# Gate and value projections of a gated FFN written as Strassen block products over pairs of token chunks

## The chip, the core and the metric

The kernel runs on one core of a Trainium2 chip: one TensorE (PE, with its weight loads PEld), one VectorE (DVE), one ScalarE (ACT), one GpSimd (POOL), and DMA queues fed from SyncE (SP). The metric is the device time of one execution in microseconds. Three executions of the kernel before took 867.61, 870.18 and 871.58 us; the median, 870.18 us, is the time to beat. Faster and slower are meant against a bound of 0.5% (4.35 us).

## What is computed

A hash attention over 2 x 8 heads of 768 tokens, then a softplus FFN, then a gated FFN on 1536 tokens of width 512 with 1536 hidden columns. Only the last is changed:

```python
def _moe2_ref(x, w_gate, w_val, w_out):
    g = x @ w_gate                         # 1536x512 @ 512x1536
    silu = g * (1.0 / (1.0 + np.exp(-g)))
    val = x @ w_val
    return (silu * val @ w_out)            # 1536x1536 @ 1536x512
```

## The kernel before

**Chunks.** The tokens are handled in four chunks c = 0 to 3 of 384 tokens, two for each of the two batches b. Attention gives `xy[c]`, the first FFN (`ffn1`) turns it into the next `xy[c]`, and the gated FFN (`ffn2`) makes the output of that chunk. The hidden width of a chunk lies on partitions (512 = KD x 128, KD = 4), its 384 tokens (CN) on the free axis.

**High and low halves.** Inputs of float32 precision are held as two halves, a rounded one and a remainder. Each 128 x 128 block of a weight meets each 128 x 384 block of data three times (`three`, L1133 to L1136): high by high, high by low, low by high. In gate and value the halves are float16 (L1134, L1135, L1136); in the out-projection they are float32r (L1300, L1301, L1302; 512 columns each). So a chunk takes 12 x 2 x 4 x 3 = 288 matmuls of 384 columns for gate and value and 3 x 12 x 3 = 108 matmuls of 512 columns for the out-projection; the four chunks take 1152 and 432.

**`ffn2`, one chunk.** For each of the 12 blocks m of hidden columns, gate goes into one bank of a PSUM tile z, value into the other. ACT takes the sigmoid (L1262), DVE multiplies by gate and by value (L1268, twice), ACT makes the high half sT (L1274), POOL the low half (L1277). After 12 blocks, three token tiles f are accumulated over all 12 blocks in PSUM, copied (ACT, L1307) and stored. The PSUM rings that matter are z (2 tiles of two banks), y and pv (1 bank each), f (2 banks).

**Weights.** `piece` (L388) loads a float64 array of 128 x 1024 values and turns it into float32 with three DVE instructions (L408, L413, L419, tile w32b); `split16` measures its size (ACT, L446, a square with an accumulated sum), and makes its two halves (L452 or L458, L462); `split32` does the same for the out-projection without a scale (L486, L490). The 12 pieces of gate and value are all made before `ffn2` starts, the 6 pieces of the out-projection in its first 40 us.

**`ffn1`'s end.** Four tiles y of 128 x 384 leave PSUM for `xy[c]` in two steps, the high half by ACT (`hi`, L1228), the low half by DVE from the same bank (`lo`, L1233).

**The order.** Every piece of work is a `step` with an engine or several (`ways`), a cost, an urgency, the steps it follows, and ring slots it takes and uses. `Order.run` (L128) walks through time by these costs, places the step that can start first (the lowest urgency among those within 0.1067 us), and so fixes each engine's queue, which the chip then runs strictly in that order. A change of steps in one place can move rows elsewhere on every engine.

## Time and profile before

| | |
|---|---|
| median of three executions | 870.18 us (867.61 to 871.58) |
| the profiled execution, first to last instruction | 868.9 us |
| PE busy | 818.3 us, 94% of the span |
| DVE, ACT, POOL busy | 546.1, 441.7, 356.9 us |
| start of gate and value | 577.24 us |
| last matmul starts | 864.71 us |

The profiled execution's time outside its span is not listed; its span lies 1.3 us below the median and inside the range of the three. A PE row's duration holds the whole passage of a matmul through the array, and the next one starts long before it ends; so what a matmul costs in a stream is read from the distance between two starts, not from its duration. Idle time of the other engines costs nothing unless PE waits for them.

### The profile page before, as it was taken

What the parts mean: (1) busy time and instruction counts of PE and PEld (TensorE: products, weight loads), DVE (VectorE), ACT (ScalarE), POOL (GpSimd) and SP (SyncE); (2) the same over time, 40 slices, a digit from 0 to 9 for tenths busy, and PEclk for the clock granted to TensorE, in tenths of its full rate; (3) what the DMA queues carried; (4) which work ended last, traced back from release to release, by engine and by line L of the source; (5) the groups of instructions that cost most, each with busy time, mean ns of one, the idle gap of its engine ahead of it and who ended that gap; (6) DMA issues with size and microseconds to landing.
All of it is one profiled execution on the core that took longest, in us unless ns stands there. A gap on an engine that the chain in (4) does not pass through costs nothing. (4 is left out here: it accounts for less than half of the span.)

```text
span 868.9 us, 14539 instructions
## 1 busy us (share of the span) xinstructions
PE 818.3 (94%) x5576; PEld 530.4 (61%) x5576; DVE 546.1 (63%) x1018; ACT 441.7 (51%) x845; POOL 356.9 (41%) x361
## 2 busy tenths in 40 slices
PE   7999898889989899788999999999999999999998
PEld 3667666545555555455666666555686686677666
DVE  4778896879998678888558789889602301311220
ACT  3445465568788578885778458534302211211220
POOL 0001201669787769986778317413301201210220
PEclk9979999999999999999999999999999999999999
DMA  6224433776859896566683650445000000001001
GB/s 205 71 86 150 149 98 103 170 139 127 199 108 171 160 174 127 113 123 113 126 151 58 206 191 5 143 160 183 1 24 13 2 24 13 1 1 37 1 1 37
DMA packets 179269, 86.10 MB, mean 99 GB/s; under 512 B 141120, under 2 KB 165888, under 8 KB 179200
## 3 DMA queue, kind: packets, MB, share of 16 engines
q1 hardware_dynamic: 179200, 85.17, 41.5%
q8 instruction: 44, 0.72, 0.4%
q14 instruction: 25, 0.20, 0.1%
HBM read 47.35 MB, written 3.15 MB: 58 GB/s over the span
## 5 line engine op out<-in xcount | busy, mean ns | idle before, releaser
L1268 DVE SCALAR_TENSOR_TENSOR sg<-z,smalls,sg 128x384 f32<-128x384 f32 x96 | 59.2, 616 | 176.2 <-ACT sg L1262 174.7
L1277 POOL TENSOR_TENSOR sT<-sg,sT 128x384 fp32r<-128x384 f32 x48 | 51.3, 1069 | 213.5 <-ACT sT L1274 202.1
L929 POOL TENSOR_TENSOR P<-E,P 128x768 f16<-128x768 f32 x72 | 124.5, 1730 | 23.3 <-ACT P L916 19.8
L869 PE MATMUL z<-k,q 128*128 128x384 f32 x192 | 79.5, 543 | 3.3 <-DVE E L888 3.3
L1194 POOL TENSOR_TENSOR g<-fr,g 128x384 f16<-128x384 f32 x64 | 71.3, 1116 | 14.9 <-ACT g L1185 11.3
L1134 PE MATMUL f<-xy,w1h 128*128 128x384 f16 x192 | 62.6, 326 | 4.0 <-DVE fr L1163 1.5
L1134 PE MATMUL z<-xy,wgh 128*128 128x384 f16 x192 | 62.6, 326 | 2.1 <-DVE sg L1268 2.1
L909 ACT ACTIVATE E<-E,st 128x768 f32<-128x768 f32 x48 | 44.7, 931 | 37.3 <-DVE E L888 35.3
L1134 PE MATMUL z<-xy,wvh 128*128 128x384 f16 x192 | 62.6, 326 | 0.0
L1135 PE MATMUL z<-xy,wvh 128*128 128x384 f16 x192 | 62.6, 326 | 0.0
L1136 PE MATMUL z<-xy,wvl 128*128 128x384 f16 x192 | 62.6, 326 | 0.0
L1136 PE MATMUL z<-xy,wgl 128*128 128x384 f16 x192 | 62.6, 326 | 0.0
L1135 PE MATMUL z<-xy,wgh 128*128 128x384 f16 x192 | 62.6, 326 | 0.0
L1136 PE MATMUL f<-xy,w1l 128*128 128x384 f16 x192 | 62.6, 326 | 0.0
L1135 PE MATMUL f<-xy,w1h 128*128 128x384 f16 x192 | 62.6, 326 | 0.0
L1262 ACT ACTIVATE sg<-z,smalls 128x384 f32<-128x384 f32 x48 | 27.8, 580 | 64.2 <-PE z L1136 62.8
L966 PEld LDWEIGHTS <-PT 128*128 128x128 f16 x1296 | 46.5, 99 | 22.0 <-DMA PT<-P 12.2
L1180 DVE SCALAR_TENSOR_TENSOR fr<-fa,smalls,fr 128x384 f32<-128x384 f32 x64 | 54.4, 852 | 5.2 <-ACT fa L1177 2.3
L966 PE MATMUL pv<-v,PT 128*128 128x64 f16 x1296 | 50.2, 194 | 7.8 <-DMA PT<-P 4.9
L1300 PE MATMUL f<-woh,sT 128*128 128x512 f32 x144 | 56.6, 393 | 0.0
L1274 ACT ACTIVATE sT<-sg 128x384 fp32r<-128x384 f32 x48 | 25.0, 522 | 61.0 <-DVE sg L1268 61.0
L1301 PE MATMUL f<-wol,sT 128*128 128x512 f32 x144 | 56.1, 389 | 0.0
(207 smaller groups left out, 2036.6 us busy)
## 6 DMA issues: line engine op xcount, KB each, us to landing
raw64a<-in_moe_w_in_dram SPq DMA_DIRECT2D x16, 512.0 KB, 4.6
raw64a<-in_moe_w_out_dram SPq DMA_DIRECT2D x16, 512.0 KB, 5.0
raw64b<-in_moe_w_gate_dram SPq DMA_DIRECT2D x12, 512.0 KB, 4.4
raw64b<-in_moe_w_val_dram SPq DMA_DIRECT2D x12, 512.0 KB, 4.9
raw64b<-in_moe_w_out_dram SPq DMA_DIRECT2D x12, 512.0 KB, 4.0
rawk<-in_k_dram SPq DMA_DIRECT2D x19, 192.0 KB, 2.9
rawv<-in_v_dram SPq DMA_DIRECT2D x19, 192.0 KB, 3.0
rawq<-in_q_dram SPq DMA_DIRECT2D x16, 192.0 KB, 3.1
```

The lines of the kernel that those rows point to most:

```text
L869: nc.tensor.matmul(a[:, x, 0:HS], lhsT=plain(qd["q"])[:, ts], rhs=plain(kd["k"])[:, x * HS:(x + 1) * HS], start=True, stop=True,)
L929: return lambda: eng.tensor_tensor(P.t[:, 1, :], E.t.rearrange("p a b -> p (a b)"), P.t[:, 0, :], op=ALU.subtract)
L966: nc.tensor.matmul(pv.t[:, t, :], lhsT=PT.t[:, w, kk, :], rhs=values.t[:, kk, c0:c0 + D], start=(kk == 0 and w == 0 and c0 == 0), stop=(kk ...
L1134: nc.tensor.matmul(ps, lhsT=wh, rhs=xh, start=first, stop=False)
L1135: nc.tensor.matmul(ps, lhsT=wh, rhs=xl, start=False, stop=False)
L1136: nc.tensor.matmul(ps, lhsT=wl, rhs=xh, start=False, stop=last)
L1180: nc.vector.scalar_tensor_tensor(out=fr.t, in0=fa.t, scalar=sc[b]["sg"], in1=fr.t, op0=ALU.mult, op1=ALU.add)
L1194: return lambda: eng.tensor_tensor(g.t[:, 1], fr.t, g.t[:, 0], op=ALU.subtract)
L1268: return lambda: nc.vector.scalar_tensor_tensor(out=sg.t, in0=z.t[:, j, 0:CN], scalar=gvs[b, "gv"[j]][:, gi:gi + 1], in1=sg.t, op0=ALU.mul ...
L1277: return lambda: eng.tensor_tensor(sT.t[:, 1, :], sg.t, sT.t[:, 0, :].bitcast(F32), op=ALU.subtract)
L1300: nc.tensor.matmul(ps, lhsT=s[:, 0, cs], rhs=wh, start=(kk == 0), stop=False)
L1301: nc.tensor.matmul(ps, lhsT=s[:, 0, cs], rhs=wl, start=False, stop=False)
```

## The change

`ffn2` is replaced by `pair_of`, which handles the two chunks of a batch (p = 0, 1) and two blocks of hidden columns (mp = 0 to 5) at once: a 2 x 2 block product for gate and one for value. Each is made from 7 products (p1 to p7 in the code) instead of 8. A product is 6 matmuls of 384 columns (2 blocks of depth x `three`). The sums that go with it are made in four places.

- **Of the data, once for each batch** (`parts7`): `ffn1`'s y is kept as float32 in one step (`keep_a` or `keep_v`). Then 8 squares with sums on ACT, a total, 4 scalings, 4 subtractions and 7 splits into halves, all on arrays of 128 x 768.
- **Of the weights, for each of 12 pieces** (`split7`): 4 sums of 128 x 256 on POOL (tile sw), and the halves of 2048 instead of 1024 values. The pieces live in a ring of 4 (w7), those of the out-projection in a ring of 2 (wo); so from mp = 2 on they are made while `pair_of` runs.
- **Of the products.** Each of gate and value has a PSUM tile A of ring z (two banks, a and c) and one bank more, y or pv. In bank a, p1, p6, p7 and p4 are added one upon the other, and after each of the first three ACT copies the running sum out to SBUF (`keep`, tile cc). Bank c takes p5 and later p3, the third bank p2. DVE adds a bank to a copy (`plus`: c11, c22, c12). So p6 waits for the first copy, p7 for the second, p4 for the third, p3 for c22.
- **Of the output.** A pair's out-projection covers two hidden blocks only (6 matmuls for each of 6 token tiles), and is added to an array acc in SBUF (DVE; 12 first copies by ACT and DVE, 60 adds). It is issued behind the products of a later pair. The stores come with mp = 5.

A pair is thus 14 products and 6 out-products of 6 matmuls each. There are 12 pairs, in the order (0,0), (0,1), (1,0), (1,1), (0,2), (1,2) and so on; all of it counts 1008 matmuls of 384 columns and 432 of 512.

```diff
+        "raw64a": 1, "w32a": 2, "raw64b": 2, "w32b": 2, "sw": 1, "w7": 4, "wo": 2,
+        "fa": 2, "fr": 2, "g": K1, "cc": 10, "sg": 4, "sT": 8,
     }
     order = Order(RINGS)
...
+    def yf(c):
+        return xy[c].rearrange("p a k n -> p (a k n)").bitcast(F32).rearrange("p (k n) -> p k n", k=KD)
...
-            def hi(mt=mt, y=y):
+            def keep_a(mt=mt, y=y):
...
-            def lo(mt=mt, y=y):
...
-            a = step(U["f1"], "A", act(CN), hi, [s, y_ready], uses=[y])
-            done.append(step(U["f1"], "V", stt(CN), lo, [a], uses=[y]))
-        return done
...
+            last.append(s)
+            done.append(ways(U["f1"], [("A", act(CN), keep_a), ("V", dve(CN) + 0.13, keep_v)], [s, y_ready], uses=[y]))
+        return done, last
...
+    def parts7(p, opened, y_ready):
...
+        def sub(o, x, y, after):
+            def go(eng):
+                return lambda: eng.tensor_tensor(f[o](), f[x](), f[y](), op=ALU.subtract)
+            return ways(u, [("W", dve(n) + 0.05, go(nc.vector)), ("G", gps(n) + 0.15, go(nc.gpsimd), BV["lo"])], after)
...
+            s = ways(u, [("A", act(n), hi_a), ("G", gts(n) + 0.08, hi_g), ("W", dve(n, 2), hi_v)], after)
+            s = ways(u, [("G", gps(n) + 0.05, lo(nc.gpsimd)), ("W", dve(n) + 0.07, lo(nc.vector))], [s])
...
+        u = -1.0 if p else 200.0
...
+        s11, s21, s12, s22 = (scaled(j) for j in ("11", "21", "12", "22"))
+        b11, b21, b22 = halves("11", [s11] + after), halves("21", [s21] + after), halves("22", [s22] + after)
+        t1 = sub("t1", "12", "11", [s11, s12] + after)
+        h1 = halves("t1", [t1])
+        t3 = sub("t3", "22", "12", [t1, s22])
+        halves("t3", [t3])
+        t2 = sub("t2", "22", "t1", [h1, s22])
+        h2 = halves("t2", [t2])
+        t4 = sub("t4", "21", "t2", [t2, b21])
+        h4 = halves("t4", [t4])
+        return out, ready, [b11, b22, h2, h4, ready["t3"]], known
...
+            def sums(eng):
...
+                    eng.tensor_tensor(o[:, 0], a21, a22, op=ALU.add)
+                    eng.tensor_tensor(o[:, 1], o[:, 0], a11, op=ALU.subtract)
+                    eng.tensor_tensor(o[:, 2], a11, a21, op=ALU.subtract)
+                    eng.tensor_tensor(o[:, 3], a12, o[:, 1], op=ALU.subtract)
...
+            raw = s
...
+            g = step(due, "-", 0.0, make, [raw], takes=[slot], line="w7")
+            s = step(due, "A", act(n) + 0.24, measure, [g], uses=[w32, slot])
+            s, bank_ = total(due, m, 1, [s])
+            sc_ = step(due, "V", 0.6, scale(bank_), [s], uses=[bank_])
+            sm = ways(due, [("G", 4 * gps(CB) + 0.2, sums(nc.gpsimd)), ("W", 4 * dve(CB) + 0.1, sums(nc.vector), BV["lo"])], [raw],
+                      takes=[sw], uses=[w32])
+            done = []
...
+    def pair_of(p, mp, gw, wo, f2_open, y7, y7_ready):
...
+            def prod(k, wj, name, bank, first, after, takes=(), uses=(), line=None):
+                return step(due + k + 0.5 * i, "E", cost, mult(wj, 0, name, bank, first),
+                            [w_done[wj // 4], y7_ready[name], w_scale[b]] + after, takes=takes, uses=[w7] + list(uses), line=line)
...
+            def keep(slot, after, A=A, sc_=sc_):
+                def go():
+                    nc.scalar.activation(new(late["f2"], [128, CN], F32, slot), A.t[:, 0, 0:CN], AF.Copy, scale=sc_[:, mp:mp + 1])
+                return step(0, "A", act(CN), go, after + [f2_open], takes=[slot], uses=[A], line="cc")
...
+            def plus(slot, bank, after, uses, sc_=sc_):
+                def go():
+                    nc.vector.scalar_tensor_tensor(
+                        out=slot.t, in0=bank(), scalar=sc_[:, mp:mp + 1], in1=slot.t, op0=ALU.mult, op1=ALU.add
+                    )
+                return step(0, "V", stt(CN) + 0.08, go, after, uses=[slot] + uses)
+            s1, u2, u3 = Slot("cc"), Slot("cc"), Slot("cc")
+            p1 = prod(0, 0, "11", bank_a, True, [f2_open], takes=[A], line="u1")
+            p5 = prod(1, 4, "t1", bank_c, True, [p1], uses=[A])
+            k1 = keep(s1, [p1])
+            p6 = prod(2, 5, "t2", bank_a, False, [k1], uses=[A])
+            p2 = prod(3, 2, "21", bank_b, True, [p1], takes=[Bk], line="u2")
+            k2 = keep(u2, [p6])
+            p7 = prod(4, 6, "t3", bank_a, False, [k2], uses=[A])
+            k3 = keep(u3, [p7])
+            c11 = plus(s1, bank_b, [p2, k1], [Bk])
+            c22 = plus(u3, bank_c, [p5, k3], [A])
+            p4 = prod(5, 3, "t4", bank_a, False, [k3], uses=[A])
+            p3 = prod(6, 7, "22", bank_c, False, [c22], uses=[A])
+            c12 = plus(u2, bank_c, [p3, k2], [A])
+            ends[i] = [c11, c12, p4, c22]
+            tiles[i] = [s1, u2, A, u3]
...
+            def mul(eng, t, sg=sg):
+                return lambda: eng.tensor_tensor(sg.t, t.t, sg.t, op=ALU.mult)
+
+            def mul_raw(n, t, sg=sg):
+                return lambda: nc.vector.scalar_tensor_tensor(
+                    out=sg.t, in0=t.t[:, 0, 0:CN], scalar=gvs[b, n][:, mp:mp + 1], in1=sg.t, op0=ALU.mult, op1=ALU.mult
                 )
...
+            for n, t, e in (("g", tg, None), ("v", tv, ends[1][j])):
+                if raw:
+                    s = step(0, "V", stt(CN) + 0.08, mul_raw(n, t), [s, e], uses=[t, sg])
+                else:
+                    s = ways(0, [("W", dve(CN), mul(nc.vector, t), 0.3), ("G", gps(CN) + 0.1, mul(nc.gpsimd, t))], [s, e], uses=[t, sg])
...
+                s = step(due + 105, "E", pe(6 * DM), mm, [pairs[0][1], pairs[1][1], wo_done], takes=[f],
+                         uses=[pairs[0][0], pairs[1][0], wo_slot])
...
+                if mp == 0:
+                    s = ways(0, [("V", dve(DM), first_v), ("A", act(DM) - 0.08, first_a)], [s], uses=[f])
+                else:
+                    s = step(0, "V", dve(DM) + 0.1, add, [s, sums_of[c, i]], uses=[f])
+                sums_of[c, i] = s
+                if mp == NG2 - 1:
+                    step(0, "D", (0.7, 0.73), store, [s])
...
+    f2_open = step(0, "-", 0.0, open_f2, [s for c in range(NCH) for s in y_last[c]])
...
+    turns_of = [(0, 0), (0, 1), (1, 0), (1, 1)]
+    turns_of += [(p, mp) for mp in range(2, NG2) for p in range(B)]
+    for p, mp in turns_of:
+        pair_of(p, mp, gws[mp], wos[mp], f2_open, y7[p], y7_ready[p])
```

What the queues become is shown at two places. The first is DVE's queue as gate and value start. Before, it holds the rest of the last weight piece (w32b, wvl), four scale steps, two pieces of the out-projection, and the multiplications of the first blocks (sg):

```order
L462 SCALAR_TENSOR_TENSOR wvl_5924<-w32b_1185_6826,smalls_87,wvh_5923 128x4x256
L1420 TENSOR_SCALAR smalls_87<-smalls_87 128x6 x4
L408 TENSOR_SCALAR w32b_1191_6928<-raw64b_1189_6922 128x1024
L413 SCALAR_TENSOR_TENSOR w32b_1191_6928<-raw64b_1189_6922,w32b_1191_6928 128x1024
L419 SCALAR_TENSOR_TENSOR w32b_1191_6928<-raw64b_1189_6922,w32b_1191_6928 128x1024
L408 TENSOR_SCALAR w32b_1194_6959<-raw64b_1190_6925 128x1024
L1268 SCALAR_TENSOR_TENSOR sg_1193_6957<-z_1188_6897,smalls_87,sg_1193_6957 128x384
L413 SCALAR_TENSOR_TENSOR w32b_1194_6959<-raw64b_1190_6925,w32b_1194_6959 128x1024
L1268 SCALAR_TENSOR_TENSOR sg_1193_6957<-z_1188_6897,smalls_87,sg_1193_6957 128x384
```

Now the same place holds the second batch's data sums (xy2 and xy3 are its two chunks, ty a scratch array), whose first instruction is the reduction L1309 eight rows ahead of these. The first `plus` of a product bank (cc) comes behind them:

```order
L1274 TENSOR_TENSOR ty_5907<-xy3_2434,xy2_2433 128x768
L1290 TENSOR_TENSOR xy0_131<-xy2_2433,xy0_131 128x768 x2
L1274 TENSOR_TENSOR xy3_2434<-xy3_2434 128x768
L1675 TENSOR_SCALAR smalls_87<-smalls_87 128x1
L1676 TENSOR_TENSOR smalls_87<-smalls_87 128x1
L1675 TENSOR_SCALAR smalls_87<-smalls_87 128x1
L1676 TENSOR_TENSOR smalls_87<-smalls_87 128x1
L1675 TENSOR_SCALAR smalls_87<-smalls_87 128x1
L1676 TENSOR_TENSOR smalls_87<-smalls_87 128x1
L1468 SCALAR_TENSOR_TENSOR cc_1174_6843<-y_1177_6867,smalls_87,cc_1174_6843 128x384
L1290 TENSOR_TENSOR xy1_132<-ty_5907,xy1_132 128x768
L1290 TENSOR_TENSOR y3_6816<-xy3_2434,y3_6816 128x768
L1468 SCALAR_TENSOR_TENSOR cc_1180_6898<-z_1171_6818,smalls_87,cc_1180_6898 128x384
```

Counted from L1309, 17 rows now stand ahead of the first cc row: four small ones for the scales, one conversion of a weight piece (L408), two scalings, two casts, and then those shown. Two more rows of 768 values stand between the first cc row and the second.

The second place is PE's queue where one hidden block or pair gives way to the next. Before, value's last matmul of a block is followed by gate's first of the next, which goes to the other slot of ring z:

```order
L1135 MATMUL z_1188_6897<-xy0_131,wvh_5923 128x384
L1136 LDWEIGHTS wvl_5924
L1136 MATMUL z_1188_6897<-xy0_131,wvl_5924 128x384
L1134 LDWEIGHTS wgh_5921
L1134 MATMUL z_1192_6932<-xy0_131,wgh_5921 128x384
L1135 LDWEIGHTS wgh_5921
L1135 MATMUL z_1192_6932<-xy0_131,wgh_5921 128x384
```

Now at the change from pair (0,1) to pair (1,0), the last product of value (z_1206) is followed at once by the first of the next pair, which takes the PSUM tile of gate (z_1189 before it, z_1225 now):

```order
L1135 MATMUL z_1206_7087<-y7_5906,w7_1194_7015 128x384
L1136 LDWEIGHTS w7_1194_7015
L1136 MATMUL z_1206_7087<-y7_5906,w7_1194_7015 128x384
L1134 LDWEIGHTS w7_1085_5995
L1134 MATMUL z_1225_7217<-xy0_131,w7_1085_5995 128x384
L1135 LDWEIGHTS w7_1085_5995
L1135 MATMUL z_1225_7217<-xy0_131,w7_1085_5995 128x384
```

At the change from pair (1,4) to pair (0,5), two out-products (f) stand between, of which the second is shown:

```order
L1537 MATMUL f_1457_8862<-wo_1395_8404,sT_1426_8627 128x512
L1538 MATMUL f_1457_8862<-wo_1395_8404,sT_1426_8627 128x512
L1539 MATMUL f_1457_8862<-wo_1395_8404,sT_1426_8627 128x512
L1537 MATMUL f_1457_8862<-wo_1395_8404,sT_1437_8715 128x512
L1538 MATMUL f_1457_8862<-wo_1395_8404,sT_1437_8715 128x512
L1539 MATMUL f_1457_8862<-wo_1395_8404,sT_1437_8715 128x512
L1134 LDWEIGHTS w7_1398_8437
L1134 MATMUL z_1459_8875<-y7_5906,w7_1398_8437 128x384
```

Ring z has 2 slots and a pair takes both, so the first product of a pair now always waits for the tile of the pair just finished. From pair (0,2) on two or three out-products stand in that place (one ahead of pair (1,2)); none stands ahead of pairs (0,1), (1,0) and (1,1).

## Rows read from the trace of the kernel before

**Rows 1.** The page's first part: busy time, share and instructions by engine.

```profile
PE 818.3 (94%) x5576; PEld 530.4 (61%) x5576; DVE 546.1 (63%) x1018; ACT 441.7 (51%) x845; POOL 356.9 (41%) x361
```

**Rows 2.** Busy time by stretch, from the start of gate and value.

```profile
core 0: us, PE busy (x) PEld busy (x) DVE busy (x) ACT busy (x) POOL busy (x), PEclk, DMA share, GB/s
577.20:587.40 10.20, 8.08 (x52) 4.81 (x51) 9.26 (x18) 3.60 (x5) 1.12 (x1) 1.00 0.30 108
587.40:626.20 38.80, 38.80 (x239) 23.28 (x239) 32.66 (x39) 15.98 (x26) 14.33 (x11) 1.00 0.26 94
...
651.00:865.10 214.10, 214.10 (x1189) 145.02 (x1188) 44.49 (x72) 45.02 (x81) 35.85 (x36) 1.00 0.03 12
```

**Rows 3.** What PE waited for, 440 to 592 us and 380 to 450 us.

```profile
PE z L1134 <- DVE sg L1268: 2.1, 1, 2.1
PE z L1134 <- DVE fr L1163: 1.1, 1, 1.1
...
PE y L1134 <- DVE xy L1233: 3.7, 1, 3.7
```

**Rows 4.** Timeline: gate's first matmul, two streams of matmuls, the end.

```profile
577.24 0.32 PE L1134 MATMUL z<-xy,wgh 128*128 128x384 f16 x1
...
838.00 0.33 PE L1134 MATMUL z<-xy,wgh 128*128 128x384 f16 x1
...
840.27 0.33 PE L1136 MATMUL z<-xy,wvl 128*128 128x384 f16 x1
...
840.90 0.39 PE L1302 MATMUL f<-woh,sT 128*128 128x512 f32 x1
...
849.53 0.39 PE L1301 MATMUL f<-wol,sT 128*128 128x512 f32 x1
...
864.71 0.39 PE L1302 MATMUL f<-woh,sT 128*128 128x512 f32 x1
865.18 0.59 ACT L1307 COPY ob<-f 128x512 f32<-128x512 f32 x1 [7.61 <-PE f L1302]
```

**Rows 5.** Groups by line and shape: busy us, mean ns, idle before them.

```profile
L1268 DVE SCALAR_TENSOR_TENSOR sg<-z,smalls,sg 128x384 f32<-128x384 f32 x96 | 59.2, 616 | 176.2 <-ACT sg L1262 174.7
L413 DVE SCALAR_TENSOR_TENSOR w32b<-raw64b,w32b 128x1024 int32<-128x1024 int32 x18 | 24.2, 1346 | 0.3
L408 DVE TENSOR_SCALAR w32b<-raw64b 128x1024 int32<-128x1024 int32 x18 | 13.8, 767 | 2.0 <-DMA raw64b<-in_moe_w_gate_dram 2.0
L462 DVE SCALAR_TENSOR_TENSOR wvl<-w32b,smalls,wvh 128x1024 f16<-128x1024 f32 x6 | 7.7, 1278 | 0.8 <-POOL wvh L458 0.8
L490 DVE TENSOR_TENSOR wol<-w32b,woh 128x1024 fp32r<-128x1024 f32 x6 | 7.3, 1218 | 0.6 <-ACT woh L486 0.6
L377 DVE TENSOR_SCALAR smalls<-smalls 128x1 int32<-128x1 int32 x12 | 1.8, 153 | 0.4
L1262 ACT ACTIVATE sg<-z,smalls 128x384 f32<-128x384 f32 x48 | 27.8, 580 | 64.2 <-PE z L1136 62.8 <-POOL sT L1277 1.2
L916 ACT CAST P<-E 128x768 f16<-128x768 f32 x44 | 36.3, 826 | 25.4 <-DMA PT<-P 25.1 <-ACT E L909 0.3
L486 ACT ACTIVATE woh<-w32b 128x1024 fp32r<-128x1024 f32 x6 | 6.3, 1055 | 8.8 <-DVE w32b L419 8.8
L446 ACT ACTIVATION_READ_ACCUMULATOR wgh<-w32b 128x1 f32 x6 | 1.1, 187 | 0.0
L1262 ACT ACT_TABLE_LOAD x1 | 1.3, 1283 | 3.5 <-DVE smalls L1420 3.5
L1277 POOL TENSOR_TENSOR sT<-sg,sT 128x384 fp32r<-128x384 f32 x48 | 51.3, 1069 | 213.5 <-ACT sT L1274 202.1 <-issue 11.4
```

**Rows 6.** By tile: shortest, median and longest duration (ns), first and last start.

```profile
L413 DVE SCALAR_TENSOR_TENSOR w32b<-raw64b,w32b x18: 1214/1226/2020, 487.1 to 613.7; 128x1024 int32<-128x1024 int32 x18
L1277 POOL TENSOR_TENSOR sT<-sg,sT x48: 993/994/1625, 588.0 to 843.3; 128x384 fp32r<-128x384 f32 x48
```

**Rows 7.** A stretch in attention with a lower granted clock, columns as in rows 2.

```profile
290.00:300.00 10.00, 7.27 (x51) 4.00 (x50) 5.28 (x14) 5.61 (x13) 6.94 (x8) 0.83 0.87 155
```

346 lines of the change are left out of this document (241 added, 105 removed), and 1 row of the table RINGS.

## Prediction

> **What bounds the kernel now.** I read four views in turn. The page's first part shows PE busy for 94% of the span and no other engine above 63% [rows 1]. An average says little of one stage, so the second view is the busy time by stretch: from 587.4 to 626.2 and again from 651 to the end PE is busy in every microsecond, at the full granted clock (1.00, that is 2.4 GHz), while DVE, ACT and POOL work for only 45, 45 and 36 of the last 214 us [rows 2]. Only the first 10 us of the stage have a gap of 2.1 us: gate's second block waits for a tile that DVE empties [rows 3]. So the stage is a stream of matmuls, and its price is their count by their pitch. The timeline gives the pitch: 14 starts of 384-column matmuls lie 2.27 us apart in all, 0.162 us each, and 38 starts of 512-column ones 8.63 us, 0.227 each [rows 4]. Then 1152 x 0.162 + 432 x 0.227 = 186.9 + 98.1 = 285.0 us, with the gap 287.1; the stage really lasts from 577.24 to the last matmul's end, 864.71 + 0.23 = 864.94, that is 287.7 us [rows 4]. The account closes to 0.6 us. The profiled span is 868.9 us, 1.3 below the median of 870.18; I work out a difference on the span and carry it to the median.
>
> **What is removed.** 144 matmuls of 384 columns of the stage's 1152: 144 x 0.162 = 23.4 us. The out-projection keeps its 432. What is left is 163.5 + 98.1 = 261.6 us. In these units a product is 6 x 0.162 = 0.97 us, an out-product 1.36 us, a pair 14 x 0.97 + 6 x 1.36 = 21.8 us.
>
> **What is mixed.** Out-products now alternate with products, some 72 changes of kind. At one such change the timeline has 0.63 us from the last 384-column start to the third 512-column start, where one step of 0.162 and two of 0.227 make 0.616 [rows 4]; 0.014 us a change gives 1.0 us.
>
> **What is added on the other engines, over some 270 us.** All durations are from the groups [rows 5]; other widths in proportion. DVE: 72 cc sums and 24 multiplications from PSUM at 0.616 (59.2), 27 multiplications of 0.46 (12.3), 60 adds of 512 columns at 0.82 (49.3), 18 low halves at 1.28 (23.0), 14 weight pieces at 0.77 + 2 x 1.35 (48.4; the third instruction is priced as the second), some 63 small ones at 0.153 (9.6), 9 us of the second batch's sums: 211 us. ACT: 168 copies, sigmoids and high halves of 384 columns at 0.58 (97), 30 weight instructions at 1.06 (32), the rest 13: 142 us. POOL: 93 instructions of 384 columns at 1.07 (99.5), 36 weight sums at 0.71 (26), 7 of 1024 columns at 2.85 (20): 145 us. None passes PE's 262, so PE stays the bound on average. What decides is the waits within the chains, which the mean does not show.
>
> **Data sums of the first batch.** Eight squares, a total and some 24 instructions of 768 values, 22 to 27 us of DVE at most. They fall in the time in which PE runs chunk 2's 192 matmuls into y, 31 us, and DVE is relieved there of 8 of the 12 gate and value pieces of 3.46 us. Hidden, 0; without that cover they would cost up to 25 us. ffn1's y now leaves its bank in one step, not two. Before, that bank once waited 3.7 us for the low half behind DVE's queue [rows 3]; I take 1.5 of it back, between 0 and 3.7.
>
> **The entry: the largest stall.** The second batch's sums stand at the head of DVE's queue, and the first cc sums behind them. I count by hand from t = 0, the end of ffn1's last matmul. ACT must still empty the last bank (0.58), split an out-projection piece (1.06) and square (0.77): 2.6 with a hand-off of 0.2 (the end of the old kernel shows 0.24 between PE's last matmul and ACT [rows 4]). PE multiplies three products and the total: 3.1. DVE's four small ones end at 4.0. Then come L408 (0.77), two scalings and two casts (4 x 0.58), four of two inputs (4 x 0.91, from L490's 1.22 for 1024), six small ones (0.93): 11.7. The first cc sum, gate's c11, ends at 12.3. Two low halves follow (14.1), gate's c22 (14.7), value's c11 (15.3), a subtraction (16.2), value's c22 (16.8). Value's last product p3 waits for this one, so pair (0,0) ends at 17.8. Its products are worth 13.6: 4.2 us lost. PE has no other work to put there, since no out-product exists yet.
>
> Pair (0,1) needs the tile of gate, which is free after gate's raw multiplication. DVE still has ahead of that a subtraction and a low half (18.6), gate's c12 (19.2), a low half (20.1), value's c12 (20.7); it ends at 21.4. With the hand-off PE starts at 21.6: 3.8 us more. Within the pair p6 and p7 wait for copies behind sizes and casts on ACT's queue, 0.9 and 1.35. At the turn to (1,0) nothing stands between the last product and the tile's next use: c12 0.62, one piece instruction ahead of it 1.3, raw multiplication 0.62 and the hand-off: 2.7. The turn to (1,1) is spared, since value's p3 stands earlier in its order. (1,2) has one out-product for it: 1.2. Of the eight later turns each has two or three out-products, 2.7 us or more, against a chain of 0.62 + 0.62 + 0.24 and one instruction of DVE that happens to run, 2.1: covered, with 0.6 to spare. A slip of 0.4 each, 3.2. The bounds of these turns: nothing, or 1.3 each (an L413 whole), 10.
>
> **A clock fall.** The stage before never waited. In attention, where PE was busy for 7.27 of 10 us, the granted clock was 0.83 [rows 7], between its two levels (1.2 and 2.4 GHz). The entry has similar gaps. One such stretch costs 0.17 x 10 = 1.7 us; I take one (bounds 0 to 5).
>
> **The end.** The last products' chain is covered by the six out-products of the previous pair, 8.2 us; then an add of 0.82 stands where a copy of 0.59 stood [rows 4], and the stores come in the last 16 us. 0.
>
> **Sum.** Waits: 4.2 + 3.8 + 2.2 + 2.7 + 1.2 + 3.2 + 1.7 = 19.0 (bounds 8 to 30: entry as low as 8 if the casts and pieces run beside each other, as high as 15 with the turns at 10 and the clock at 5). Stage: 261.6 + 1.0 + 19.0 = 281.6 against 287.7, 6.1 less, with y 7.6 less: 870.2 - 7.6 = 863.
>
> **The rivals.**
>
> (A) Slower: DVE and POOL hold each other up. L413 took 1.23 us in the median, 2.02 at the longest; POOL's multiplication 0.99 and 1.63 [rows 6]. POOL goes from 36 us in 214 to 145 in 262, and some 80 DVE instructions have both inputs in SBUF. If that makes the instruction ahead of the release chain 0.8 to 1.5 us longer, each turn loses 1 us or more beyond the 0.6 to spare, and the keeps and cc sums within a pair slip with it. It decides from 7.6 / 12 = 0.6 us a pair; at 1 us a pair the time is 875. Against it: the links themselves (c12, raw multiplication) read one input from PSUM, and such a group, L1268, shows a mean of 616 ns beside a POOL at work [rows 5]. The Trainium skill, "SBUF — State Buffer", section "SBUF: two separate sides", calls the port pair that VectorE (with two SBUF inputs) and GpSimd share an exclusive lock, held for a whole instruction, with the loser blocked. By that rule a DVE instruction could wait a whole 1.07 us; the longest L413 above, 0.8 over its median, agrees with it.
>
> (B) Faster: ACT and DVE run the entry with more overlap than I let them, the turns cost nothing and the clock holds. Waits of 8: 261.6 + 1.0 + 8 = 270.6, 17.1 less, with y 852. For it: the copies and cc sums are short (0.58 and 0.62 us), and DVE and ACT have a third of the stage free; against it: each queue runs strictly in its order, and the entry's order is bad for the cc sums.
>
> (C) No change: the waits eat the gain. Six clock falls of 1.7 in place of one, or turns at 1.3 each, add 8 to 10: 868 to 874. For it: six waits within each pair (copies, cc sums) have a slack of one or two products, 1 to 2 us, less than one weight instruction on ACT (1.06) plus a sigmoid and the table load of 1.28 [rows 5].
>
> **Chances.** The forecast 0.50 with its own range 857 to 869, B 0.20, C 0.17, A 0.13. The bound of 0.5% is 4.35 us, about what a measurement here tells from no change: under 865.8 is faster, over 874.5 slower. Faster: 0.40 of the forecast's half and B, 0.60. Same: 0.10 of the forecast, C and a little of A, 0.29. Slower: the rest of A, 0.11. The range goes from B's 852 to 873; below and above it stay about 2 in 10.
>
> **What would show it.** Right: gate and value start near 577; a pitch of 0.162 and 0.227 unchanged; the first cc sum on DVE some 12 us after the start; PE's waits, some 15 us of them in the first 50 us of the stage, by ACT's and DVE's cc and DVE's sg; later turns with out-products and next to no wait; a clock of 1.00 but for a slice or two. Wrong: waits at every turn, or L413 and POOL's multiplications far longer than here (A); many slices under 1.00 (C); no wait after 590 (B); or a later start of the stage, which would mean that the first batch's sums are not hidden. The likeliest error is in the count of the entry, since each of its steps depends on the one before it.

## The result and the profile after

The changed kernel takes 878.53 us in the median of seven executions (874.79 to 883.32), the kernel before 870.18: the ratio is 1.0100, 95% interval 1.0069 to 1.0131. It is slower by 1%, and lies above the forecast of 863 and above the range's end at 873. The profiled execution took 882.55 us, with a span of 880.6. Ratios and intervals here are made from undisturbed executions alone (one of the run with the first sums late took 1613.9 us and is left out) and can differ by a few thousandths from the ratio of the medians; beside the experiments the kernel before had medians of 868.8 to 870.0.

The first view is the page's first part, against [rows 1]. PE works 6.5 us less, DVE 108 us more.

```profile
PE 811.8 (92%) x5436; PEld 517.1 (59%) x5436; DVE 653.8 (74%) x1188; ACT 501.9 (57%) x966; POOL 473.1 (54%) x453
```

The timeline of PE has the places that answer to [rows 4]: gate's first matmul, the longest wait of the stage with what follows it, and the end.

```profile
586.28 0.33 PE L1134 MATMUL z<-y,w 128*128 128x384 f16 x1
...
605.00 0.33 PE L1136 MATMUL z<-y,w 128*128 128x384 f16 x1
609.45 0.48 PE L1134 MATMUL z<-y,w 128*128 128x384 f16 x1 [4.13 <-DVE sg L1505]
609.73 0.53 PE L1135 MATMUL z<-y,w 128*128 128x384 f16 x1
...
701.82 0.32 PE L1134 MATMUL z<-y,w 128*128 128x384 f16 x1 [1.93 <-DVE cc L1468]
701.98 0.32 PE L1135 MATMUL z<-y,w 128*128 128x384 f16 x1
...
876.44 0.39 PE L1539 MATMUL f<-wo,sT 128*128 128x512 f32 x1
```

Gate and value start 9.0 us later than before (586.28 against 577.24) and last from there to 876.67, 290.4 us against 287.7. So about half of this execution's distance to the forecast lies ahead of the stage. Busy time by stretch (columns as in [rows 2]) shows two stretches ahead of it, then the three that answer to [rows 2], shifted by 9:

```profile
500.00:540.00 40.00, 40.00 (x249) 24.10 (x247) 38.03 (x44) 25.94 (x50) 24.11 (x20) 1.00 0.20 64
560.00:580.00 20.00, 20.00 (x125) 12.05 (x124) 0.16 (x1) 2.39 (x6) 1.43 (x2) 1.00 0.00 1
586.20:596.40 10.20, 9.34 (x60) 5.61 (x59) 6.77 (x14) 7.34 (x12) 5.43 (x2) 1.00 0.01 2
596.40:635.20 38.80, 29.89 (x152) 18.16 (x151) 36.45 (x48) 19.93 (x33) 26.36 (x20) 0.91 0.25 82
660.00:874.10 214.10, 208.01 (x1119) 139.80 (x1118) 159.27 (x242) 91.87 (x163) 117.48 (x106) 1.00 0.15 50
```

DVE is nearly full in 500 to 540 (38.0 of 40 us) and empty in 560 to 580 (0.16 of 20). In the 39 us of the entry PE works only 29.9 us. What PE waited for, first from 451 to 586 us, then in the stage (us in all, times, longest), against [rows 3]:

```profile
PE f L1134 <- DVE smalls L371: 1.4, 1, 1.4
PE f L359 <- DVE fr L1166: 1.3, 1, 1.3
PE f L359 <- ACT w L1354: 1.3, 1, 1.3
PE z L1134 <- DVE fr L1166: 1.0, 2, 0.7
PE pv L966 <- DMA PT<-P: 0.9, 1, 0.9
```

```profile
PE z L1134 <- DVE sg L1505: 6.6, 2, 4.1
PE z L1134 <- DVE cc L1468: 4.2, 5, 1.9
PE z L1134 <- ACT cc L1463: 3.9, 5, 1.2
PE f L1537 <- DVE acc L1553: 2.6, 3, 1.3
PE f L1537 <- DVE acc L1547: 0.7, 1, 0.7
PE f L359 <- ACT w L1354: 0.3, 1, 0.3
```

Counted from start to start, as below, each wait is some 0.17 us longer than its idle time. The stage's 290.4 us are then: matmuls at the pitches of the prediction 262.7 (with ten totals, each two small matmuls that add up the squares of a weight piece), 17 waits 21.3, matmuls at the lower clock 3.2 more than at the full one (12 from 609.45 on and 10 from 637.94 on, each behind a wait of 4.1 and 2.5 us), changes between products and out-products about 1, small rests about 2 (the pitch at 512 columns is 0.230 us here, not 0.227, which makes some 1.2 of them).

### The profile page after: what moved, and what is told of

Read it like the earlier page. It is cut to its first block, busy times and chain, and to the rows that moved or that the text cites. A ratio compares the mean times of both kernels' runs of the same rounds, so it can differ in the third digit from the quotient of the medians.

```text
span 880.6 us, 14652 instructions
## 1 busy us (share of the span) xinstructions
PE 811.8 (92%) x5436; PEld 517.1 (59%) x5436; DVE 653.8 (74%) x1188; ACT 501.9 (57%) x966; POOL 473.1 (54%) x453
## 4 chain that ended last, share of the span: by engine, by line
PE 46%; DVE 27%; DMA 12%; POOL 5%; issue 5%; ACT 3%; SPq 1%; DVEq 0%; POOLq 0%; ACTq 0%
DMA PT<-P 7%; PE z L1134 5%; PE z L1136 5%; PE z L1135 5%; PE z L869 4%; PE f L1537 3%; PE f L1539 3%; PE f L1538 3%; PE f L602 3%; DVE fr L1183 2%; PE pv L966 2%; DMA raw64a<-in_moe_w_in_dram 2%; POOL P L929 2%; DVE E L888 2%; DVE fr L1166 2%
## 5 line engine op out<-in xcount | busy, mean ns | idle before, releaser
L1502 POOL TENSOR_TENSOR sg<-cc,sg 128x384 f32<-128x384 f32 x45 | 51.0, 1144 | 69.8 <-DVE cc L1468 32.9
L1134 PE MATMUL z<-y,w 128*128 128x384 f16 x216 | 71.4, 331 | 12.3 <-DVE cc L1468 4.2
L1197 POOL TENSOR_TENSOR g<-fr,g 128x384 f16<-128x384 f32 x64 | 67.1, 1055 | 17.3 <-ACT g L1188 13.2
L1463 ACT ACTIVATE cc<-z,smalls 128x384 f32<-128x384 f32 x72 | 40.4, 576 | 55.2 <-PE z L1136 54.9
L1513 POOL TENSOR_TENSOR sT<-sg,sT 128x384 fp32r<-128x384 f32 x48 | 59.8, 1263 | 21.4 <-ACT sT L1510 21.4
L1136 PE MATMUL z<-y,w 128*128 128x384 f16 x216 | 71.2, 330 | 0.0
L1135 PE MATMUL z<-y,w 128*128 128x384 f16 x216 | 71.2, 330 | 0.0
L1134 PE MATMUL f<-xy,w1h 128*128 128x384 f16 x192 | 63.9, 333 | 2.5 <-DVE smalls L371 1.4
L1537 PE MATMUL f<-wo,sT 128*128 128x512 f32 x144 | 62.2, 432 | 3.3 <-DVE acc L1553 2.6
L1135 PE MATMUL f<-xy,w1h 128*128 128x384 f16 x192 | 64.0, 333 | 0.0
L966 PEld LDWEIGHTS <-PT 128*128 128x128 f16 x1296 | 47.4, 100 | 25.2 <-DMA PT<-P 15.2
L1539 PE MATMUL f<-wo,sT 128*128 128x512 f32 x144 | 56.4, 392 | 0.0
L1538 PE MATMUL f<-wo,sT 128*128 128x512 f32 x144 | 56.3, 391 | 0.0
L888 DVE TENSOR_SCALAR_CACHE_REDUCE E<-z 128x768 f32<-128x768 f32 x48 | 45.5, 953 | 14.5 <-PE z L869 9.0
L1135 PEld LDWEIGHTS <-w 128*128 128x128 f16 x336 | 33.2, 99 | 36.7 <-issue 18.8
L1553 DVE TENSOR_TENSOR acc<-f,acc 128x512 f32<-128x512 f32 x60 | 41.2, 687 | 16.6 <-PE f L1539 14.9
```

The lines of the kernel that those rows point to most:

```text
L888: nc.vector.tensor_scalar(new(att, [128, 2, HS], F32, E), z.t[:, :, 0:HS], PLAIN_TOP, None, op0=ALU.min, op1=ALU.min, accum_out=a[:, 1:2],)
L966: nc.tensor.matmul(pv.t[:, t, :], lhsT=PT.t[:, w, kk, :], rhs=values.t[:, kk, c0:c0 + D], start=(kk == 0 and w == 0 and c0 == 0), stop=(kk ...
L1134: nc.tensor.matmul(ps, lhsT=wh, rhs=xh, start=first, stop=False, skip_group_check=onto)
L1135: nc.tensor.matmul(ps, lhsT=wh, rhs=xl, start=False, stop=False, skip_group_check=onto)
L1136: nc.tensor.matmul(ps, lhsT=wl, rhs=xh, start=False, stop=last, skip_group_check=onto)
L1197: return lambda: eng.tensor_tensor(g.t[:, 1], fr.t, g.t[:, 0], op=ALU.subtract)
```

## The experiments

All runs are measured by two stretches. The mark between attention and them is the first matmul of the second batch's first FFN into a z tile. Ahead of the mark, five kernels here have the same queues (the changed one, its repetition, the sums later, the filler, no GpSimd products), and yet the mark falls at 451.4, 444.6, 442.9, 452.0 and 446.1 us. That is scatter of attention, and it hides in every total. From the mark on, the changed kernel and its repetition agree within 0.2 us.

| run | mark to gate | stage | both | PE's waits in the stage | median, us | ratio to before (95%) |
|---|---|---|---|---|---|---|
| before | 128.7 | 287.7 | 416.4 | 2.3 | 870.18 | |
| changed | 134.9 | 290.4 | 425.3 | 21.3 | 878.53 | 1.010 (1.007 to 1.013) |
| the same again | 134.9 | 290.6 | 425.5 | 20.9 | 877.29 | 1.009 (1.006 to 1.013) |
| y in two steps | 134.8 | 290.7 | 425.5 | 21.0 | 880.42 | 1.012 (1.004 to 1.019) |
| second sums later | 135.0 | 283.9 | 418.9 | 14.2 | 872.11 | 1.004 (1.000 to 1.008) |
| no sums | 126.0 | 279.2 | 405.2 | 13.4 | 858.66 | 0.983 (0.973 to 0.993) |
| weight sums in four steps | 136.8 | 293.1 | 429.9 | 22.8 | 884.27 | 1.013 (1.004 to 1.022) |
| out-piece later | 145.5 | 287.4 | 432.9 | 19.5 | 884.52 | 1.015 (1.008 to 1.023) |
| three edits | 137.1 | 284.6 | 421.7 | 16.4 | 875.91 | 1.006 (1.001 to 1.010) |
| filler | 135.3 | 288.5 | 423.8 | 14.4 | 877.26 | 1.009 (1.005 to 1.012) |
| first sums late | 131.7 | 286.0 | 417.7 | 18.0 | 870.07 | 1.001 (0.997 to 1.004) |
| both sums late | 129.8 | 285.3 | 415.1 | 15.2 | 870.93 | 1.001 (0.999 to 1.004) |
| pieces late too | 129.2 | 293.6 | 422.8 | 25.3 | 876.69 | 1.011 (1.004 to 1.017) |
| no GpSimd products | 134.7 | 295.4 | 430.1 | 23.2 | 883.32 | 1.016 (1.010 to 1.021) |
| second value piece | 130.6 | 284.3 | 414.9 | 18.3 | 871.83 | 1.005 (1.001 to 1.010) |
| totals later | 129.9 | 288.7 | 418.6 | 22.2 | 872.42 | 1.006 (1.001 to 1.011) |
| both of these | 127.5 | 285.1 | 412.6 | 16.9 | 866.86 | 1.001 (0.997 to 1.005) |
| chain alone | 126.1 | 270.0 | 396.1 | 6.2 | 848.15 | 0.978 (0.973 to 0.984) |

**The same kernel again.**

> The changed kernel once more, unaltered, for a second profile. In the first one gate and value start 9.0 us later than before (586.3 against 577.2) and last 290.4 us against 287.7. If the late start is a property of the order, it comes back within 2 us (584 to 588), and so do the waits of the entry (4.3 us for gate's second tile, 2.7 at the first turn to the second batch). If it was an accident of that execution, the start lies near 578 and the total near 870.

The waits came back one by one, and so did the 134.9 us; the absolute start (579.5) did not, since attention ended 6.8 us earlier. So the first half of the statement holds for the stretch from the mark, and the accident lies ahead of it.

**y in two steps.** Is it the new order of attention's rows?

```diff
-            done.append(ways(U["f1"], [("A", act(CN), keep_a), ("V", dve(CN) + 0.13, keep_v)], [s, y_ready], uses=[y]))
+            def again(mt=mt, y=y):
...
+            a = step(U["f1"], "A", act(CN), keep_a, [s, y_ready], uses=[y])
+            done.append(step(U["f1"], "V", stt(CN), again, [a], uses=[y]))
```

> ffn1's y leaves its bank in two steps again, one of ScalarE and a second of VectorE, whose result goes nowhere. This adds 16 VectorE instructions of about 0.62 us to the changed kernel and gives PE the order of the kernel before up to the first data total at about 492 us. Theory 1, the late start comes from attention's rows being put in another order: the start of the third chunk's first FFN matmuls goes back from 452.6 to about 448.7, and gate and value start 3 to 5 us earlier, at 581 to 583; total 3 to 5 us less than the changed kernel. Theory 2, it comes from the first batch's data sums alone, on VectorE between 490 and 555: 448.7 is not reached again or is given back there, and the total is the same or up to 3 us more.

With PE's old order the stretch takes 134.8 us, as before this edit, so the late start from the mark on is not of that order. The mark lies at 451.2, no earlier, and the median is no lower; given the scatter of the mark, one execution does not exclude a few us ahead of it. The wait for y's bank that the kernel before had ([rows 3], 3.7 us), absent as changed, is back, as the waits from 375 to 450 us show:

```profile
PE y L1134 <- DVE junk L1239: 3.7, 1, 3.7
```

**No sums at all.** The data sums as a whole:

> Left out: all data sums (squares, total, scalings, subtractions, splits of both batches); y leaves as two halves as before, and all seven products take blocks of these halves, so that the output is another one. Everything on the weights, the products and the output stays. It gives the price of the data sums as a whole. If they cause the late start and the slow entry: start at 577 to 580, entry waits under 3 us, total 12 to 18 us under the changed kernel, that is 860 to 866, and what is left of waits belongs to the products' own chain. If the weight pieces and the chain cause the loss: start as late as in the changed kernel, total less than 5 us lower.

Ahead of the stage 8.9 us go, in the stage 11.3, together 20.2, and PE waits for nothing between mark and gate. The total fell by 20, more than expected. With the sums go the 21 one-value multiplications by the data's scale in the stage (L1676), 12.6 us of DVE as changed. The profiled execution is the longest of its four (862.54 us, the median 858.66), but from the mark to the last matmul its clock is 1.00, and the run with the chain alone, below, repeats the 126.0 (126.1). What PE still waited for in the stage:

```profile
PE z L1134 <- ACT cc L1467: 4.1, 4, 1.8
PE f L1541 <- DVE acc L1557: 2.7, 4, 1.0
PE z L1134 <- DVE cc L1472: 2.3, 4, 0.8
PE z L1134 <- DVE sg L1509: 2.1, 2, 1.7
```

**Second batch's sums later.**

```diff
-        u = -1.0 if p else 200.0
+        u = 1.0 if p else 200.0
```

> The second batch's data sums get an urgency below that of the copies and cc sums instead of above. All queues are unchanged up to the end of ffn1. Theory, the entry stands behind these sums on VectorE: the waits inside pair (0,0) (5.1 us) and at the turn to (0,1) (4.3 us) fall to 2 to 4 us together, the stretch at the lower clock behind the second one goes, and the total falls by 5 to 8 us. Rival, the sums are needed anyway and only move: the first pair of the second batch waits for them as long, or the next weight piece comes late, and the total stays within 2 us.

The stage fell by 6.6 us. The 4.3 us at pair (0,1) are gone; a new wait of 3.1 us for value's second weight piece stands 40 us into the stage.

**Weight sums in four steps, and the out-piece later.** Two ways to keep weight work out of the way:

> The four sums of a weight piece become four steps of the planner instead of one, so that other rows can stand between them; nothing else is changed. In both profiles of the changed kernel PE loses 3.1 us some 42 us ahead of gate and value, where VectorE waits 2.2 us for a low half of the first FFN on GpSimd, which stands behind four sums of 3.6 us. Theory, the weight sums block GpSimd's queue there: these waits go, and the lower clock behind them in some executions; gate and value start 130 to 132 us after the second batch's first FFN matmul instead of 134.9; total 3 to 5 us less. Rival, the data sums take the time of VectorE and ScalarE whichever way GpSimd is ordered: the waits turn up at another place, 134 to 136.

```diff
     for mp in range(NG2):
         gws.append([gv_piece(mp, w_gate, "g", e_wg), gv_piece(mp, w_val, "v", e_wv)])
-        wos.append(out_piece(mp))
+        if mp:
+            wos.append(out_piece(mp - 1))
+    wos.append(out_piece(NG2 - 1))
```

> The first out-projection piece goes behind value's second piece in the order of pieces. Before, it holds one of the two buffers w32b until ffn1 has ended, so that value's second piece cannot be made while VectorE is idle in ffn1's last 25 us and is made in the entry. Theory: its 2.7 us of conversion and 2.6 us of low halves leave the entry; the waits of the entry that remain are those of the data sums, and the total falls by 2 to 5 us. Rival: the entry waits for the data sums anyway and the out-projection piece is late now; total within 2 us.

Neither theory holds; both are slower than the rivals had it (136.8 against 134 to 136, and a total some 6 us up where the rival gave 2). In four steps the sums no longer cause the two waits at 42 us ahead of the gate, but others of 0.6 to 2.5 us stand elsewhere, 8.9 in all. With value's second piece freed the planner puts it among the FFN's rows, not into the idle time: PE's waits between mark and gate rise from 7 to 16.6 us, and the stretch to 145.5.

```profile
PE f L1134 <- DVE fr L1166: 8.4, 3, 3.6
PE f L359 <- ACT w L1354: 3.6, 2, 2.2
PE z L1134 <- DVE fr L1166: 2.1, 2, 1.3
PE pv L966 <- DMA PT<-P: 1.2, 1, 1.2
```

The FFN's activations on DVE (fr) are most of what PE waits for. The piece's 5.3 us of DVE rows (2.7 and 2.6 by the expectation) come with 10.6 us more on the stretch.

**Three edits together.**

> The second batch's sums later, the weight sums in four steps and the out-projection piece later, all three together. If they add up: the late sums give 6.6 us in the stage (283.9 against 290.5), the four steps 3 to 4 ahead of it, the piece 2 to 3, so that the time from the second batch's first FFN matmul to the last matmul is about 413 us, against 416.3 before and 425.4 as changed; total 864 to 868, 1 to 5 us under the kernel before. If they get in each other's way the sum stays over 417.

They do not add up: 421.7. The stage has the gain of the first (284.6), but ahead of it the other two lose 2.2 us.

**A filler for the clock.** Ahead of the first product of the two pairs, with nfill 24 and 14, and zb the bank of value that was read last:

```diff
+                    nfill = {(0, 1): 24, (1, 0): 14}.get((p, mp), 0) if wj == 0 and i == 0 else 0
+                    for x in range(nfill):
+                        nc.tensor.matmul(
+                            late["zb"].t[:, 0:CN], lhsT=w7.t[:, 0, 0:128], rhs=y7[name](0, 0),
+                            start=True, stop=True, skip_group_check=True)
...
```

> Added: 24 matmuls of 384 columns into a bank that is already read, ahead of the first product of pair (0,1), and 14 ahead of the first of pair (1,0), where PE waits 4.3 and 2.7 us; they need 3.9 and 2.3 us at full clock and nobody reads them. All other queues are those of the changed kernel. Theory, the halved clock behind these two places (12 and 10 matmuls at 0.32 us) comes of PE's idle time there: it stays at 1.00 and the stage takes 290.5 - 3.5 = 287 us. Rival, it comes of something else, or the granted clock falls anyway: 290 to 291.

```profile
606.24 4.06 PE L1434 MATMUL pv<-y,w 128*128 128x384 f16 x24
610.54 0.32 PE L1134 MATMUL z<-y,w 128*128 128x384 f16 x1 [0.24 <-DVE sg L1512]
```

The first product behind the filler runs at full clock (0.32 us where 0.48 and 0.53 stood), and so do those at the second place. But ten matmuls at 0.52 us now appear earlier in the entry, from 601.7 on, behind waits of at most 1.17 us that brought no fall as changed, and a total and an add wait longer (1.19 and 1.18 us); the stage gains 2.0 us, not 3.5. With PE's idle time the fall goes at the two places; what sets the moment of a fall stays open.

**First batch's sums late, then both.** The sums wait for the last row of chunk 3's first FFN (gdone holds its steps):

```diff
-    y7[0], y7_ready[0], free0, k0 = parts7(0, [opened], y_done)
+    y7[0], y7_ready[0], free0, k0 = parts7(0, [opened] + gdone[NCH - 1], y_done)
```

> The first batch's data sums (squares, total, scalings, subtractions, splits) wait for the last row of the first FFN of chunk 3, after which VectorE is idle for some 20 us in the changed kernel while PE multiplies into y. Theory, they cost their 9 us (134.9 against 126.0 without any sums, from the second batch's first FFN matmul to gate and value) because VectorE, ScalarE and GpSimd have no room for them among that FFN's own rows: the stretch falls to 126 to 129 us, the stage stays at 290 to 291, total 6 to 8 us under the changed kernel, near 870. Rival, room is short everywhere and the chain of squares, total, scaling, subtraction and split (some 20 us) is late for gate's first product: 131 to 140.

> The first batch's data sums behind chunk 3's FFN, and the second batch's with an urgency below that of the copies and cc sums. If both add up: 126 to 129 us ahead of gate and value and 284 to 285 for the stage, together 410 to 414 against 416.3 in the kernel before; total 864 to 868, faster than before by 2 to 6 us. If the second batch's sums come to lie in VectorE's way once more, the stage stays at 290.

The first alone takes 3.2 us from the stretch ahead and 4.4 from the stage. Its 131.7 us lie in the rival's range (131 to 140), at the near end; the total is the theory's, by a gain in the stage that the theory did not have. The busy time of the stretches that answer to 500 to 540 and 560 to 580 as changed, counted from the mark, shows the work moved out of the crowded time (DVE 28.95 of 40 us instead of 38.03) into the idle one (13.77 of 20 instead of 0.16):

```profile
493.30:533.30 40.00, 39.18 (x244) 23.58 (x243) 28.95 (x39) 22.95 (x44) 24.07 (x28) 1.00 0.25 84
553.30:573.30 20.00, 20.00 (x126) 12.18 (x125) 13.77 (x25) 8.90 (x17) 0.92 (x1) 1.00 0.00 1
```

Both together come to 415.1, 1.3 under the kernel before; in the totals that is no difference.

**More pieces late.** As the last run, with the reordering of the out-piece (above) and:

```diff
-            Gv(), "b", src, (0, KD), mp * G2, G2, split7(slot, e), U["gw"] + 10.0 * mp, [opened], line="pc"
+            Gv(), "b", src, (0, KD), mp * G2, G2, split7(slot, e), U["gw"] + 10.0 * mp, [opened] + (gdone[NCH - 1] if mp else []), line="pc"
```

> As the run with both sums late, and also: the pieces from the second hidden block on wait for chunk 3's FFN, and the first out-projection piece goes behind value's second. Theory, chunk 3's FFN is free of weight work and the idle time of VectorE takes it: 126 to 127 us ahead of the stage, and in the stage the 3.1 us wait for value's second piece goes: 280 to 283; together 406 to 410. Rival, sums and two pieces (25 us of VectorE together) do not both fit in 25 us, and the first product waits: 130 or more ahead of the stage.

The rival was right about the room, though not about the place: not the first product waits but a total of value's second piece, 36 us into the stage, for 8.1 us.

```profile
609.36 0.59 PE L359 MATMUL f<-smalls 128*128 128x1 f32 x2 [8.13 <-ACT w L1357]
```

**No products on GpSimd.** This was meant as the test of rival A:

```diff
-                    s = ways(0, [("W", dve(CN), mul(nc.vector, t), 0.3), ("G", gps(CN) + 0.1, mul(nc.gpsimd, t))], [s, e], uses=[t, sg])
+                    s = ways(0, [("W", dve(CN), mul(nc.vector, t), 0.3)], [s, e], uses=[t, sg])
```

> All 72 multiplications of copies and sums by the sigmoid are done by VectorE; in the changed kernel GpSimd does 45 of them. GpSimd falls by about 50 us in the stage, VectorE rises by some 25. Theory of contention (VectorE's instructions with two inputs in SBUF last 1.2 to 2.0 us beside GpSimd, and this is what PE's waits in the later pairs come from): their means fall towards 1.22, the waits after the first 60 us fall from 9 us to under 4 and the stage to 284 to 286. Rival, the later waits are those of a queue in a fixed order: VectorE is fuller, the waits stay or grow, stage 290 to 296.

The stage takes 295.4 us, 5 more. Four groups of DVE in the stage of this run, where the low halves from w32b (L1386) and the one-value multiplications (L1676) stand beside the two that the expectation is about:

```profile
L1502 DVE TENSOR_TENSOR sg<-cc,sg 128x384 f32<-128x384 f32 x72 | 43.1, 613 | 3.1 <-ACT sg L1499 2.9
L413 DVE SCALAR_TENSOR_TENSOR w32b<-raw64b,w32b 128x1024 int32<-128x1024 int32 x14 | 18.3, 1315 | 0.1
L1386 DVE SCALAR_TENSOR_TENSOR w<-w32b,smalls,w 128x1024 f16<-128x1024 f32 x9 | 17.2, 1916 | 0.0
L1676 DVE TENSOR_TENSOR smalls<-smalls 128x1 f32<-128x1 f32 x21 | 13.5, 644 | 0.7
```

The same groups as changed:

```profile
L413 DVE SCALAR_TENSOR_TENSOR w32b<-raw64b,w32b 128x1024 int32<-128x1024 int32 x14 | 20.3, 1453 | 0.1
L1502 DVE TENSOR_TENSOR sg<-cc,sg 128x384 f32<-128x384 f32 x27 | 17.6, 662 | 3.0 <-ACT sg L1499 3.0
L1386 DVE SCALAR_TENSOR_TENSOR w<-w32b,smalls,w 128x1024 f16<-128x1024 f32 x9 | 14.1, 1567 | 0.0
L1676 DVE TENSOR_TENSOR smalls<-smalls 128x1 f32<-128x1 f32 x21 | 12.6, 601 | 0.7
```

Two means fall, two rise. I take as stretch what a DVE row lasts beyond the shortest of its line and shape in that execution, for all rows of the stage that are more than 0.1 us over: 27.4 us here, 28.4 as changed. So the edit gave DVE 45 rows more and left the contention almost as it was. The fuller queue is slower, as the rival had it; what the contention costs, this run does not tell.

**Value's second piece, the totals, and both,** each on top of the run with both sums late. The first takes the reordering of the out-piece (above) and lets value's second piece alone wait for chunk 3's FFN; the second puts an empty planner step of 1.5 us between a piece's square and its total.

> As the run with both sums late, and also: the first out-projection piece behind value's second piece in the order of pieces, and value's second piece behind chunk 3's first FFN. With both sums late the largest wait left is 3.75 us, 39.5 us into the stage, for this piece. Theory: it is made in VectorE's idle time while PE multiplies into y, the wait goes, 281 to 283 for the stage, 129 to 131 ahead of it, together 411 to 413 against 416.3 before; total 864 to 867. Rival, the first batch's sums lie in the same idle time and become late for gate's first product: together 415 to 420.

> As the run with both sums late, and also: the planner places a weight piece's total on PE 1.5 us later than it did. Totals that stand in PE's queue before their square on ScalarE has ended cost 1.36 + 0.99 us ahead of the stage and 0.57 in it. Theory: these 2 to 3 us go, together 412 to 413; total 866 to 869. Rival, the later totals only make the pieces later: 415 to 418.

> The two edits before this one together. If they add up: 408 to 411 from the second batch's first FFN matmul to the end, total 861 to 866, faster than before by 4 to 9 us. If the planner's new order undoes one of them: 412 to 418.

Singly neither gains: 414.9 and 418.6 against 415.1. The first takes the 3.75 us wait away and has 2.8 and 2.1 us in the entry instead, the second has more waits in the stage (22.2). Together they give 412.6, at the near end of what was expected if one edit undoes the other, and less than either alone would suggest. This is the best order found, 3.8 us under the kernel before from the mark on, but the total's ratio is 1.001 (0.997 to 1.005): not faster by what can be told.

**The chain alone.** Besides what the run without sums leaves out:

```diff
-    for mp in range(NG2):
+    for mp in range(2):
         gws.append([gv_piece(mp, w_gate, "g", e_wg), gv_piece(mp, w_val, "v", e_wv)])
         wos.append(out_piece(mp))
+    gws, wos = gws * (NG2 // 2), wos * (NG2 // 2)
```

> Left out: all data sums (as in the run without them), and the weight pieces from the third hidden block on; the pieces of the first two blocks are used again, so that the output is another one. PE's matmuls, the copies, cc sums, multiplications, splits of sT and adds to acc all stay. It gives what the products' own chain costs. Without data sums the stage took 279.2 us, of which 13.4 are waits. Theory, the later waits come from weight pieces on VectorE and ScalarE between the chain's rows: waits fall to 5 to 8 us, stage 271 to 274. Rival, they are the chain's own (a copy or cc sum between two products on one bank): waits 11 to 14, stage 277 to 279.

```profile
PE z L1134 <- ACT cc L1467: 2.3, 3, 1.0
PE z L1134 <- DVE sg L1509: 2.1, 2, 1.7
PE z L1134 <- DVE cc L1472: 0.8, 1, 0.8
```

Six waits are left, 6.2 us, all in the first 42 us. From then on the products' own chain never makes PE wait. The theory holds, with the stage (270.0) just below its 271: later waits, those for acc included, come with the weight pieces, whose rows here end early (those of the out-projection too).

## Why the prediction was wrong

From the mark to the end the runs give one account: 416.4 before; 396.1 with the products and their chain alone, which is 20.3 less; 9.2 more with the weight pieces in the stage (405.2, no sums); 8.9 more for data sums ahead of the stage and 11.3 more for them in it, 425.3. The two parts were taken out in one order only, so the split between them holds for that order. The arithmetic saving is real, and more than all of it is given back by work on the other engines.

**The step that failed first: "Data sums of the first batch ... Hidden, 0".** They cost 8.9 us (134.9 against 126.0 without sums), nearly all of it visible at PE between mark and gate: 6.9 us of waits and 1.7 lost at the lower clock in the profiled execution, 8.6 of waits in the repetition, and neither without sums. A later start is the sign that the prediction itself named for this. I named as cover PE's 31 us of matmuls into y and the pieces that DVE no longer makes. But these sums ran while DVE, ACT and POOL served chunk 3's first FFN (DVE 38.0 of 40 us busy, POOL 24.1), and DVE's idle time came after they were done. Moving them there gave back 3.2 us alone and, with the second batch's sums, the piece and the totals moved as well, 7.4 (127.5). That DVE's fullness by itself makes the waits is not shown. In the kernel before, the same 40 us from the mark have DVE almost as full, with POOL at 15.3, and PE waited 1.2 us between mark and gate:

```profile
497.20:537.20 40.00, 40.00 (x253) 24.54 (x252) 36.02 (x55) 27.97 (x50) 15.29 (x17) 1.00 0.32 107
```

Nor is it POOL's load by itself: in the same 40 us of the best order found (both of these) POOL has 24.5 and DVE 27.8, and PE waits 1.4. It takes the two together, or an unlucky order of their rows; the runs do not part these. The relief was worth 2.7 us (128.7 to 126.0). Net, the stage started 6.2 us later from the mark, where the sum, with 1.5 us for y's bank, had it earlier. The bank's wait of 3.7 us did go, but PE's waits from 375 to 450 us are 8.6 us in all against 5.7 before, so the 1.5 shows in no time.

**The entry** was right in its places and nearly in its sizes. The first cc sum ended 12.9 us after the start, against 12.3; part of that nearness is luck, since one row ahead of it (L1676) lasted 1.35 us where the count had 0.16, and the others together came out shorter. Pair (0,0) lost 5.1 us against 4.2, the turn to (0,1) 4.3 against 3.8, the turn to (1,0) 2.7 against 2.7. The copies in pair (0,1) cost 1.0 rather than 2.2.

**The later turns and the adds: mis-sized.** I gave the turns 4.4 us and the adds nothing; behind the turn to (1,0) PE waited 7.4 us, 3.1 of them for adds to acc and 0.4 for a total; an add before it cost 0.8. The weight pieces were in the prediction as DVE's load (211 us forecast, 218 measured over the stage in the repetition), and a load below PE's was taken to be harmless. The runs without and with them differ by 9.2 us, 7.2 of them waits. The ten totals, which the forecast's sum left out, are another 1.1.

**The clock: mis-sized.** One fall at 1.7 us was forecast; there were two in the stage (3.2 us) and, in this execution, one ahead of it (1.7).

**The rivals.** C said that the waits eat the gain, 868 to 874, which is the right kind, in a size too small and for causes (turns, several clock falls) that are only part of it. A's 875 comes nearest to the time, and its mechanism is there: the stretch of 28.4 us, of which 3.1 lie in the 16 us of DVE's queue before the end of the longest wait (4.1 us) and 3.0 in those before the wait of 1.9 at 701.82. Its links behaved as the argument against it said (the cc sums kept their 613 ns). It is not the whole cause: the chain alone has 7.9 us of stretch and no wait after the first 42 us. What it cost PE stays open, as no run takes the contention away and leaves the rest. B's overlap did not come about. The range ended at 873 because the first batch's sums, priced at "up to 25" without their cover, were left out of its bounds.

**Right:** the pitches (0.162, and 0.230 against 0.227), 262.7 us of matmuls with the totals against 261.6 without, the changes of kind (about 1 us), and the end without a wait. Two slips weigh nothing: 1152 x 0.162 is 186.6 and not 186.9, and the stage before did wait once, 2.1 us, at a clock of 1.00.

## What to carry to other kernels

Saved matmuls are worth their pitch only as far as the work that pays for the saving makes PE wait for nothing. Long matmul work on PE is no cover by itself: look first for idle time in the rows of the engines that do the added work, in that stretch. A full row is a warning and not yet a wait, as the kernel before shows. Take the added work away piece by piece (no sums, then chain alone) before tuning its order; here these two runs split the loss, while most edits of order moved waits from place to place. An edit that is to test a contention must be read in all groups that it could touch, since here two fell while others rose. In a kernel whose order comes from a planner, place new work by a dependency on the row that ends the crowded time, since an urgency only decides among rows that are ready.
